# A scatter of mirrored rows that starts at partition 1 and moves 112 rows in place of 113

## The chip, the cores and the metric

The kernel runs on one core of a Trainium2 chip. The metric is the device time of one execution in microseconds. Before the change the median of three runs is 688.1 us (683.28 to 690.54).

## The reference

Eight batches, 12 heads, 448 rows, head width 64, model width 768, hidden width 3072. What is computed, cut to its core:

```python
scores = scale * np.matmul(q, k.transpose(0, 1, 3, 2))
attn = np.maximum(scores, 0.0) ** 2 / S
x = (attn @ v)                      # then heads side by side: (8, 448, 768)
X = np.fft.fft(np.fft.fft(x, axis=1), axis=2)
u = x + np.real(X)
un = (u - mean(u)) / np.sqrt(var(u) + 1e-06)
out = u + np.maximum(un @ w_ch1, 0.0) @ w_ch2
```

Inputs and output are float32; the kernel's matmuls take bfloat16.

## The kernel before

Work goes through eight batches b = 0 to 7. For each batch TensorE (PE) makes scores (`psS`, L734), ScalarE and VectorE turn them into squares (`sq`), PE multiplies by the values (L716), the result is copied to `xT`, folded, and sent through the Fourier matrices (L1210, L1024). Meanwhile PE works on the feed-forward part of earlier rows: first layer at L1445 (`hT <- unT, w`), second layer at L1496 and L1576, whose partial sums VectorE adds into the output tile `o` (L1431). The order of all instructions on each engine is fixed while the program is built, by a planner (`Streams.run`) that knows due times and costs; on the chip each engine then works through its list in that order, so an instruction that waits holds up everything behind it on its engine.

The Fourier result of a real signal is symmetric: rows s and 448 - s come from the same products. So `mix_rows` makes two tiles of rows at a time: `us[0]` holds rows s, `us[1]` holds their mirror images 448 - s. For batches 2 to 7 (`b >= PAR`) it goes over the even rows first (ch = 0, partition p is row 2p, 113 of them with rows 0 and 224) and then over the odd rows (ch = 1, 112 of them). The top half of a batch goes to `utop` (float32, for the output sum) and `ntop` (bfloat16, normalised, for the first layer); the mirrored half goes to `ubot` and `nbot`, in DRAM. Those tiles have 384 rows, of which 224 are used.

The mirrored rows come in reverse order, so they are written by a scatter: an indirect DMA issued by GpSimd (POOL) at L1120 in `store_rows`, whose destination row for each partition stands in a small index tile, `back2[ch]` (`backe` in the profile). The top rows go out by a plain DMA from SP at L1117. Partition 0 of the even mirrored tile is row 448, which is the mirror of row 0 and is not part of the output: its index is 224, an unused row.

From batch 1 on, the mirrored tile `u` has one buffer for both ch (`side` gives 1), and so do the `un` tiles. So the first instruction that writes the next `u` (POOL, L1057, then L1059) waits until the scatter out of that buffer has landed, and the next `un` (L1082 on POOL or L1085 on ACT) waits for the `nbot` scatter. Behind POOL's L1057 and L1059 stand the row statistics on VectorE (L1066), and behind those in VectorE's list the additions and copies that free PE's accumulators.

Before a batch's rows go to the first layer, SP reads them back transposed (`unT <- ntop`, `unT <- nbot`, L1158); SP's one list also holds the transposes of q and k (L481), of `xT` (L650), the loads `o <- utop`, `o <- ubot` (L1363) and the stores of the output (L1367).

Of the kernel before, what the change touches and what calls it, by code (L numbers as in the profile page):

```python
# [136 lines left out]
def need(eng, dur, deps=(), bufs=(), ok=None):  # L137
    return eng, dur, list(deps), list(bufs), ok
# [26 lines left out]
def kernel(  # L165
# [9 lines left out]
    nc = tc.nc  # L175
# [3 lines left out]
    R = S // 4  # L179
    HS = S // 2  # L180
# [12 lines left out]
    PAR, EV = 2, 113  # L193
# [39 lines left out]
    back2 = [const.tile([128, 1], mybir.dt.int32, name=f"backe{i}") for i in range(2)]  # L233
# [31 lines left out]
    def mirrors():  # L265
        order[0] = work.tile([128, 128], BF16, name="order", tag="qkr0", bufs=1)
        nc.gpsimd.memset(rev, 0.0)
        nc.gpsimd.affine_select(out=rev, in_=rev, compare_op=ALU.not_equal, fill=1.0,
                                base=-127, pattern=[[1, 128]], channel_multiplier=1)
        nc.gpsimd.iota(back[0], pattern=[[0, 1]], base=HS, channel_multiplier=-1)  # L270

        v = const.tile([128, 2], FP32, name="backv")
        nc.gpsimd.iota(v[:, 0:1], pattern=[[0, 1]], base=HS - 128, channel_multiplier=-1,
                       allow_small_or_imprecise_dtypes=True)
        nc.gpsimd.tensor_scalar(v[:, 1:2], v[:, 0:1], 0.0, float(UB), op0=ALU.is_lt, op1=ALU.mult)
        nc.gpsimd.tensor_tensor(v[:, 0:1], v[:, 0:1], v[:, 1:2], op=ALU.add)
        nc.gpsimd.tensor_copy(back[1], v[:, 0:1])
        for i in range(2):
            nc.gpsimd.iota(back2[i], pattern=[[0, 1]], base=HS - i, channel_multiplier=-2)
        nc.gpsimd.memset(order[0], 0.0)  # L280
        for i in range(2):
            n = EH - i
            nc.gpsimd.affine_select(out=order[0][:, i * EH:i * EH + n], in_=order[0][:, i * EH:i * EH + n],
                                    compare_op=ALU.not_equal, fill=1.0, base=-i, pattern=[[-2, n]],
                                    channel_multiplier=1)
        nc.gpsimd.tensor_scalar(order[0][:, EH - 1:EH], order[0][:, EH - 1:EH], 0.5, None, op0=ALU.mult)
# [75 lines left out]
    def load_group(i, which=(0, 1, 2)):  # L362
# [3 lines left out]
        for x, (nm, src) in enumerate((("q", q), ("k", k), ("v", v))):  # L366
            if x not in which:
                continue
            if b == 0 and x < 2:
                e = yield need("POOL", 0.85)  # L370
                t = first_qk[x][:R, g]
            else:
                e = yield need("POOL", 0.85, bufs=[BQ[x] if x == 2 else BQ[x][home(i)]])
                t = work.tile([R, HG, 4 * Dh], BF16, name=f"{nm}n",
                              tag="vn" if x == 2 else f"{nm}n{home(i)}", bufs=3 if x == 2 else 1)
            nc.gpsimd.dma_start(out=t, in_=src[b, hs].rearrange("h (p j) d -> p h (j d)", j=4))  # L376
            loads[i][x] = t.rearrange("p h (j d) -> p j h d", j=4)

            ready[i][x].t = sch.dma(e, GRP, 360e3, "sw") + (1.5 if g else 0.0, 3.0, 14.0, 7.0)[min(b, 3)]
            if i == 0 and x == 1:  # L380
                yield need("POOL", 0.7)
                make_identity(nc, ident)
            if i == 0 and x == 2:
                e = yield need("POOL", 1.1)
                dft_indices()
                indices_ready.t = e + LATENCY["POOL"]
            if i == 2 and x == 2:
                yield need("POOL", 0.75)
                pads()
            if i == NG + 1 and x == 1:  # L390
                yield need("POOL", 3.6)
                mirrors()
# [716 lines left out]
    def store_rows(b, ch, top, bot, us, nbytes, t, cells):  # L1109

        get = lambda u: u() if callable(u) else u
        s0, s1 = SC[ch]
        n = s1 - s0 if b < PAR else EV - ch
        w = min(128, HS - s0) if b < PAR else R
        if top is not None:
            e = yield need("SP", 0.1, [t[0]])
            nc.sync.dma_start(out=top[s0:s0 + w, :] if b < PAR else top[ch::2, :], in_=get(us[0])[:w])  # L1117
            cells[2 * ch].t = sch.dma(e, w * D * nbytes)
        e = yield need("POOL", 1.1, [t[1]])
        nc.gpsimd.indirect_dma_start(  # L1120
            out=bot, out_offset=bass.IndirectOffsetOnAxis(ap=(back if b < PAR else back2)[ch][:n], axis=0),
            in_=get(us[1])[:n], in_offset=None)
        cells[2 * ch + 1].t = sch.dma(e, w * D * nbytes) + 1.0

    def u_store(b, ch, us, ut, freed):
        yield from store_rows(b, ch, utop[b], ubot[b], us, 4, ut, u_stored[b])
        yield need("SP", 0.0, freed)
        for i in range(2):
            t = max(u_stored[b][2 * ch + i].t, freed[i].t)
            BU[i][side(b, ch)].free.append(t)  # L1130
            if b == ONE - 1 and ch == 0:
                u_left[i].t = t

    def n_store(b, ch, t):
        yield from store_rows(b, ch, ntop[b], nbot[b], [lambda i=i: uns[b][2 * ch + i] for i in range(2)], 2,
                              t, n_stored[b])
        if b > 0:
            BUN[0].free.append(n_stored[b][2 * ch + 1].t)
# [571 lines left out]
```

## Time and profile before

| | |
|---|---|
| median of three runs | 688.1 us (683.28 to 690.54) |
| the profiled execution | 686.53 us |
| its span, first to last instruction | 684.6 us |
| PE busy | 594.1 us |
| VectorE busy | 408.0 us |
| ScalarE busy | 331.2 us |
| GpSimd busy | 153.4 us |
| mean granted clock of TensorE | 0.945 |

Shares and chains below are of the profiled execution. Busy time of an engine counts instructions that run, not those that wait.

### The profile page before, as it was taken

Reading aid. Unit: us, or ns where it says so; the run is one execution under the profiler, and the core shown is the slowest. Engines: PE = TensorE matmul, PEld = TensorE weight load, DVE = VectorE, ACT = ScalarE, POOL = GpSimd, SP = SyncE. Lnnn points to the kernel's source line nnn. Section 1 sums busy time; section 2 is a strip of 40 time slices with the busy share of each in tenths; the row PEclk is TensorE's granted clock in tenths of the full one; section 3 lists DMA queues with packets and bytes.
Section 4 is the critical chain, followed back from the end, with each engine's and each line's share of the span. In section 5 each row is a group of like instructions: output and inputs, shape, how many; then the busy total and the mean of one; then the engine's idle time right before and its main releaser. Section 6 shows DMA issues by size and latency. Waiting matters only on the chain.

```text
span 684.6 us, 11457 instructions
## 1 busy us (share of the span) xinstructions
PE 594.1 (87%) x4476; PEld 371.7 (54%) x4476; DVE 408.0 (60%) x929; ACT 331.2 (48%) x503; POOL 153.4 (22%) x190
## 2 busy tenths in 40 slices
PE   8999999999748999479988699599689936999997
PEld 6575565444414455137645467258347724777684
DVE  6977779776547477366857576578546713232313
ACT  5858736765123577255575538366434302122130
POOL 8360314111232112331414133203300221000000
PEclk9999999999969899799998999899989977999999
DMA  9999997877359869999799959994783322312021
GB/s 134 210 217 224 223 141 180 116 120 110 99 72 134 153 133 63 73 158 189 117 76 128 223 110 88 144 200 94 37 148 86 90 75 57 111 35 81 24 70 47
DMA packets 141941, 81.96 MB, mean 120 GB/s; under 512 B 86054, under 2 KB 137158, under 8 KB 141888
## 3 DMA queue, kind: packets, MB, share of 16 engines
q1 hardware_dynamic: 93120, 47.50, 41.4%
q0 software_dynamic: 48768, 33.74, 34.0%
q8 instruction: 35, 0.57, 0.3%
q14 instruction: 18, 0.15, 0.1%
HBM read 62.91 MB, written 26.27 MB: 130 GB/s over the span
## 4 chain that ended last, share of the span: by engine, by line
PE 42%; DMA 28%; issue 16%; DVE 4%; POOL 4%; ACT 4%; SPq 2%; POOLq 0%; DVEq 0%; ACTq 0%
PE psF L1445 20%; DMA ubot<-u,backe 16%; PE psF L1576 10%; DMA nbot<-un,backe 7%; PE psF L1470 3%; PE psS L734 3%; PE psF L716 3%; ACT sq L759 2%; DMA qkT<-qkr 2%; DMA unT<-ntop 1%; DMA ntop<-un 1%; DMA o<-ubot 1%; POOL u L1057 1%; POOL u L1059 1%; DVE sq L774 1%
## 5 line engine op out<-in xcount | busy, mean ns | idle before, releaser
L1445 PE MATMUL psF<-unT,w 128*128 128x256 bf16 (+2 forms) x1728 | 238.9, 298 | 36.9 <-ACT hT L1419 17.1
L1445 PEld LDWEIGHTS <-w 128*128 128x128 bf16 x1728 | 169.7, 100 | 103.7 <-issue 37.3
L759 ACT ACTIVATE sq<-psS 112x896 bf16<-112x896 f32 x192 | 164.2, 917 | 57.1 <-PE psS L734 56.8
L1419 ACT ACTIVATE hT<-psF 128x512 bf16<-128x512 f32 (+3 forms) x166 | 86.0, 530 | 134.2 <-PE psF L1445 133.6
L1576 PEld LDWEIGHTS <-hT 128*128 128x128 bf16 x792 | 78.3, 100 | 77.3 <-issue 31.5
L774 DVE TENSOR_TENSOR sq<-sq 112x896 bf16<-112x896 bf16 x162 | 98.6, 623 | 20.7 <-ACT sq L759 19.6
L1576 PE MATMUL psF<-w,hT 128*128 128x384 bf16 x462 | 83.7, 333 | 3.5 <-DVE hT L1417 3.5
L1431 DVE TENSOR_TENSOR o<-psF,o 128x384 f32<-128x384 f32 x92 | 50.7, 551 | 48.5 <-PE psF L1576 42.1
L1066 DVE BATCH_NORM_STATS2 stats<-u 112x6 f32<-112x384 f32 (+2 forms) x56 | 29.1, 546 | 62.1 <-POOL u L1057 52.0
L734 PE MATMUL psS<-qkT 64*128 64x448 bf16 (+1 forms) x384 | 54.2, 373 | 5.6 <-DMA qkT<-qkr 3.6
L716 PE MATMUL psF<-sq,vn 112*64 112x448 bf16 x312 | 38.7, 372 | 14.2 <-DVE o L1431 14.2
L1576 PE MATMUL psF<-wsum,hT 128*128 128x384 bf16 x198 | 38.5, 347 | 14.5 <-DVE o L1431 14.5
L1057 POOL TENSOR_TENSOR u<-tp,xn 112x385 f32<-112x385 f32 (+2 forms) x14 | 12.8, 912 | 170.1 <-DVE tp L1039 86.8
L716 PEld LDWEIGHTS <-vn 112*64 112x64 bf16 x384 | 18.4, 112 | 42.0 <-issue 34.4
L1069 ACT ACTIVATE std<-mv,eps_t 112x1 f32<-112x1 f32 (+2 forms) x28 | 8.2, 295 | 67.7 <-DVE mv L1067 56.1
L553 DVE TENSOR_SCALAR xT<-psF 128x224 bf16<-128x224 f32 x56 | 19.2, 384 | 33.1 <-PE psF L716 33.0
L734 PEld LDWEIGHTS <-qkT 64*128 64x128 bf16 (+1 forms) x384 | 16.1, 103 | 35.0 <-issue 24.1
L376 POOL DMA_DIRECT2D qn<-in_q_dram x21 | 15.3, 731 | 85.0 <-DVE qkr L469 67.8
L1085 ACT ACTIVATE un<-u,nmr,rstd 113x768 bf16<-113x768 f32 (+2 forms) x20 | 20.1, 1022 | 23.2 <-DMA nbot<-un,backe 12.7
L376 POOL DMA_DIRECT2D vn<-in_v_dram x24 | 17.2, 718 | 58.3 <-PE psS L734 40.4
L1417 DVE TENSOR_SCALAR hT<-psF 128x512 bf16<-128x512 f32 (+3 forms) x38 | 20.4, 549 | 16.2 <-PE psF L1445 15.6
L771 ACT ACTIVATE sq<-sq 112x896 bf16<-112x896 bf16 x30 | 28.5, 954 | 0.5
(166 smaller groups left out, 658.8 us busy)
## 6 DMA issues: line engine op xcount, KB each, us to landing
out_dram<-o SPq DMA_DIRECT2D x56, 192.0 KB, 2.3
vn<-in_v_dram POOLq DMA_DIRECT2D x24, 224.0 KB, 8.0
qn<-in_q_dram POOLq DMA_DIRECT2D x21, 224.0 KB, 5.1
kn<-in_k_dram POOLq DMA_DIRECT2D x21, 224.0 KB, 7.4
w<-in_moe_w_ch_dram POOLq DMA_DIRECT2D x12, 384.0 KB, 13.9
w<-in_moe_w_ch_dram POOLq DMA_DIRECT2D x4, 1152.0 KB, 22.9
utop<-u SPq DMA_DIRECT2D x12, 336.0 KB, 5.8
o<-utop SPq DMA_DIRECT2D x16, 192.0 KB, 6.3
```

The costliest lines, as they stand in the source:

```text
L376: nc.gpsimd.dma_start(out=t, in_=src[b, hs].rearrange("h (p j) d -> p h (j d)", j=4))
L716: nc.tensor.matmul(av[h * Dh:(h + 1) * Dh, 0:S], lhsT=vn[:, c, h0 + h, :], rhs=sq[:, h, :], start=(c == 0), stop=(c == 3))
L734: nc.tensor.matmul(sc[:wide, h, 0:S].rearrange("k (c q) -> k c q", c=4), lhsT=flat[ps, k0:k0 + wide], rhs=qT[ps, m % 2], start=True, stop= ...
L759: nc.scalar.activation(r, sc[:R, :, 0:S], AF.Relu)
L771: nc.scalar.activation(r, r, AF.Square)
L774: nc.vector.tensor_tensor(r, r, r, op=ALU.mult)
L1066: nc.vector.bn_stats(stats[:n, hf, :], u[:n, hf * (D // 2):(hf + 1) * (D // 2)])
L1419: nc.scalar.activation(hs, ps, AF.Relu)
L1431: nc.vector.tensor_tensor(o, pc[:, 0:DH], o, op=ALU.add)
L1445: nc.tensor.matmul(ph[:, i * N:(i + 1) * N], lhsT=w1_sb[m][hf][:, (jj + i) * 128:(jj + i + 1) * 128], rhs=unT[:, m, 0:N], start=(m == 0), ...
L1470: nc.tensor.matmul(pc[:, 0:DH], lhsT=block(j, c), rhs=w2(j, hf), start=(j == 0), stop=(j == JC - 1))
L1576: nc.tensor.matmul(pc[:, 0:DH], lhsT=lhs[i], rhs=rhs[i], start=(start and i == 0), stop=(i == KP - 1), skip_group_check=True)
```

## The change

The even mirrored scatter leaves out partition 0, whose destination is the unused row. It reads partitions 1 to 112 of the tile, and since the index tile is read from its partition 0 on, its values are shifted by one row: 222 - 2p in place of 224 - 2p. For the odd rows the new expression gives the values that it gave before (223 - 2p), from partition 0, 112 rows. Both `ubot` and `nbot` go through this code, so in batches 2 to 7 it changes 12 scatters of 24. The rows of data that are used are the same, and so is the order of instructions on every engine.

```diff
         for i in range(2):
-            nc.gpsimd.iota(back2[i], pattern=[[0, 1]], base=HS - i, channel_multiplier=-2)
+            nc.gpsimd.iota(back2[i], pattern=[[0, 1]], base=HS - 2 + i, channel_multiplier=-2)
...
-        n = s1 - s0 if b < PAR else EV - ch
+        n, r0 = (s1 - s0, 0) if b < PAR else (R, 1 - ch)
...
             out=bot, out_offset=bass.IndirectOffsetOnAxis(ap=(back if b < PAR else back2)[ch][:n], axis=0),
-            in_=get(us[1])[:n], in_offset=None)
+            in_=get(us[1])[r0:r0 + n], in_offset=None)
```

Here `R` is 112, `HS` is 224, `EV` is 113 and `PAR` is 2.

## Rows read from the trace of the kernel before

**Rows 1.** The page, busy time, share of the span, instructions of each engine.

```profile
PE 594.1 (87%) x4476; PEld 371.7 (54%) x4476; DVE 408.0 (60%) x929; ACT 331.2 (48%) x503; POOL 153.4 (22%) x190
```

**Rows 2.** Chain that ended last, by line, shares of the span.

```profile
by line: PE psF L1445 20.2%; issue 16.0%; DMA ubot<-u,backe 15.5%; PE psF L1576 9.6%; DMA nbot<-un,backe 6.7%; PE psF L1470 2.7%; PE psS L734 2.7%; PE psF L716 2.7%; ACT sq L759 2.0%; DMA qkT<-qkr 1.7%; DMA unT<-ntop 1.4%; DMA ntop<-un 1.3%
```

**Rows 3.** Waits of POOL, then of VectorE: us in total, times, longest.

```profile
POOL u L1057 <- DMA ubot<-u,backe: 83.2, 6, 19.6
POOL un L1082 <- DMA nbot<-un,backe: 34.5, 4, 10.6
...
DVE stats L1066 <- POOL u L1057: 52.0, 6, 14.7
```

**Rows 4.** PE in order of time: start, us, instructions, [idle before <- releaser].

```profile
198.25 1.70 PE L716 MATMUL psF<-sq,vn 112*64 112x448 bf16 x8 [14.24 <-DVE o L1431]
...
223.92 2.08 PE L1445 MATMUL psF<-unT,w 128*128 128x384 bf16 x6 [3.78 <-DMA unT<-nbot]
...
286.11 4.00 PE L1576 MATMUL psF<-wsum,hT 128*128 128x384 bf16 x12 [10.06 <-DVE o L1431]
...
308.82 5.46 PE L1445 MATMUL psF<-unT,w 128*128 128x256 bf16 x36 [5.17 <-DMA unT<-ntop]
...
362.54 4.59 PE L1445 MATMUL psF<-unT,w 128*128 128x256 bf16 x24 [6.56 <-DVE xT L553]
...
431.03 2.99 PE L1576 MATMUL psF<-w,hT 128*128 128x384 bf16 x9 [3.50 <-DVE hT L1417]
...
445.14 3.59 PE L1576 MATMUL psF<-wsum,hT 128*128 128x384 bf16 x12 [4.41 <-DVE o L1431]
...
496.42 0.96 PE L716 MATMUL psS<-sq,vn 112*64 112x448 bf16 x4 [5.28 <-DVE sq L774]
505.50 2.08 PE L1445 MATMUL psF<-unT,w 128*128 128x256 bf16 x12 [2.67 <-DVE o L1431]
...
566.09 5.19 PE L1445 MATMUL psF<-unT,w 128*128 128x256 bf16 x24 [12.92 <-ACT hT L1419]
575.24 4.06 PE L1445 MATMUL psF<-unT,w 128*128 128x256 bf16 x24 [3.95 <-ACT hT L1419]
```

**Rows 5.** POOL in order of time around the first even scatter of batch 2.

```profile
173.58 2.43 POOL L1120 DMA_INDIRECT ubot<-u,backe  x1 [0.32 <-POOL u L1059]
195.24 0.90 POOL L1057 TENSOR_TENSOR u<-tp,xn 112x385 f32<-112x385 f32 x1 [19.23 <-DMA ubot<-u,backe]
...
199.83 1.04 POOL L1120 DMA_INDIRECT ubot<-u,backe  x1 [0.30 <-issue]
```

**Rows 6.** DMA issues (us to landing), 113 rows, issued near 173.6, 336.7, 489.9, 418.2.

```profile
ubot<-u,backe POOLq DMA_INDIRECT x1, 21.5
...
ubot<-u,backe POOLq DMA_INDIRECT x1, 22.5
...
nbot<-un,backe POOLq DMA_INDIRECT x1, 11.7
...
nbot<-un,backe POOLq DMA_INDIRECT x1, 21.6
```

**Rows 7.** The same, 112 rows, near 575.0, 375.6, 493.5; last batch 1's two.

```profile
nbot<-un,backe POOLq DMA_INDIRECT x1, 2.8
...
nbot<-un,backe POOLq DMA_INDIRECT x1, 6.7
...
ubot<-u,backe POOLq DMA_INDIRECT x1, 10.0
...
ubot<-u,back POOLq DMA_INDIRECT x2, 5.4
```

**Rows 8.** Busy by stretch: us, five engines, PEclk, DMA share of 16, GB/s.

```profile
190.00:195.00 5.00, 0.00 (x0) 0.00 (x0) 0.00 (x0) 0.00 (x0) 0.00 (x0) 0.50 0.06 26
```

**Rows 9.** The same, PE alone: first of ten stretches after idle, and sum.

```profile
198.25:202.40 4.15, 4.15 (x19) 0.50 0.49 122
...
505.50:509.63 4.13, 4.13 (x23) 0.59 0.59 179
...
sum 39.82, PE 39.81; mean PE 3.98
```

**Rows 10.** DMA issues from 255 to 285 us: transposes by SP in batch 3.

```profile
qkT<-qkr SPq DMA_TRANSPOSE x2, 14.5
```

## The prediction

> **What bounds the kernel now.** I read the busy table first: PE works for 594.1 us of a span of 684.6 us [rows 1], so some 90 us are PE waiting, and those are what an edit outside PE can win. The chain of waits then names a DMA where one would expect PE: the two scatters `ubot` and `nbot` of batches 2 to 7 hold 15.5% and 6.7% of the span [rows 2], together some 152 us. A share of the chain is not yet a saving, since PE works beside most of it. So I followed the wait down the engines. POOL waits 83.2 us in six pieces for `ubot`, always to overwrite the one `u` buffer, and 34.5 us for `nbot` to overwrite `un`; VectorE, whose next item is the statistics of that `u`, stands for 52.0 us in six pieces behind POOL [rows 3]. PE stops when VectorE no longer frees its accumulators: in the list of PE's idle gaps I count ten from 170 us on that hang on this [rows 4], among them 14.24, 10.06 and 12.92 us.
>
> Next, why a scatter takes so long. The even ones have 113 rows and land 20 to 22 us after issue (float32), or 11.7 us and once 21.6 us (bfloat16, half the bytes) [rows 6]. The odd ones, one row fewer and otherwise alike, land in 2.8 to 6.7 us (bfloat16), and in 10.0 us (float32) where they were issued 3.6 us behind an even `nbot` and land with it [rows 7]. A stretch where nothing else ran shows what the difference is: between 190 and 195 us all five engines are idle, the scatter is alone, and the DMA engines are busy for 0.06 of their sixteenfold time, moving 26 GB/s [rows 8]. 0.06 is one engine of sixteen. **113 rows go through one DMA engine**, 112 rows do not.
>
> **The rule beside it.** The Trainium skill, "DMA: Bandwidth & Descriptors", section on why a DMA increments its semaphore by 16 and not by 1, says that a transfer uses the largest number of engines up to 16 that divides the size of its slowest dimension. 113 is prime, so this gives one; 112 gives 16; the trace agrees for 113 with its 0.06. The same section names an exception on trn2, by which some copies issued from GpSimd spread over all engines with the count rounded up; by that 113 rows would already be spread and the sum below would be zero. The 0.06 of [rows 8] speaks against it here.
>
> **The change, part by part.**
>
> *The index tile.* One iota is replaced by another of the same shape: nothing. It is built in the first microseconds and the order of every engine is unchanged.
>
> *Issue.* An even scatter holds POOL for 2.43 us, an odd one for 1.04 us [rows 5]. Twelve even ones at odd price: 12 x 1.4 = 17 us of POOL. POOL is busy for 153 us in all [rows 1], and its time counts only through the waits below, so I add nothing for it.
>
> *Landing of the even `ubot`.* No scatter starting at partition 1 is in the trace, so this is bounded. Below: 2.8 us, an odd `nbot` of half the bytes. Above: 10.0 us, the odd `ubot` that lands together with a slow one. The nearest rows are the two of batch 1, float32 rows of the same width, 5.4 us [rows 7]. I take 7 us, since batches 2 to 7 have more transfers beside them. Should the start at partition 1 keep the scatter on one engine, it stays at 21.5; that is a rival.
>
> *What it frees.* About 14 us earlier landing, six times, is 84 us, more than the 52.0 us of VectorE's wait. Its longest piece, 14.7 us [rows 3], stands behind the scatter that took 21.5 us: it is gone at a landing under 21.5 - 14.7 = 6.8 us, so at 7 us 0.2 us remain, at 10 us 3.2 us. The other five share 37.3 us, 7.5 us each, and are gone at either.
>
> *Even `nbot`.* By the same rows, from 11.7 or more to about 4 us. It sits before the odd `un`, hence before the odd `nbot` and the transposed read of the rows.
>
> *PE's gaps.* Six follow the `ubot` scatter directly: 14.24, 10.06, 6.56, 3.50, 5.28 and 12.92 us = 52.6 us. Four follow from the later `un` and its transposes: 3.78 (`unT <- nbot`), 5.17 (`unT <- ntop`), 2.67 and 3.95 us = 15.6 us [rows 4]. Together **68.1 us**. I leave in place the 4.41 us gap at 445 us and smaller ones: there the last wait is a q/k transpose.
>
> *The clock.* After each of these gaps PE restarts at a granted clock of 0.50, the lower of its two levels (1.2 GHz in place of 2.4): ten stretches, 39.8 us of work, nine at about 0.50 and one at 0.59 [rows 9]. At full clock the same work takes half of it, less 0.4 us for the one: **19.5 us**.
>
> *Given back.* What is late next is SP's list. In batch 3 the q/k transposes already take 14.5 us to land [rows 10], and the two gaps on `unT` (3.78 + 5.17 us) end on transposes. I let half of these two stay, 4.5 us, with 2 us of slow clock behind them, and 1.5 us for the residue of `ubot`: **8 us**.
>
> Sum, from the profiled execution's own 686.5 us (span 684.6): 686.5 - 68.1 - 19.5 + 8 = **607 us**. That execution is 1.6 us under the median of 688.1, which is inside the spread of the three runs. With no gap given back it would be 599; if the small gaps went too, some 590. I take 607, with 592 to 622 as this case's own range.
>
> **The rivals.**
>
> 1. *Only the direct waits go.* The scatter spreads, but SP's queue is what comes next: the four following gaps stay, and each batch gains a new wait of 2 us on a transpose. For it: rows 10, and that the scatter now uses all the engines that the transposes use. Against: other stretches with the same list of work show PE nearly without gaps, and the planner's order assumed quick scatters. Time: 686.5 - 52.6 - 15 (their part of the clock, 52.6/68.1 of 19.5) + 12 = 631 us. Chance 0.17.
>
> 2. *It doesn't spread.* The start at partition 1, or the shifted pairing of index and row, leaves the scatter on one engine, or the count wasn't the reason. Then nothing but one row in 113 is saved: 0.2 us of each landing, 686 us. Against it stands that the odd scatters differ in nothing else but the count. Chance 0.05. The Trainium skill's exception, above, would give the same time.
>
> 3. *Slower.* Spread over all sixteen engines, an even scatter gets ahead of q/k and `xT` transposes on every engine instead of one, and the score matmuls (L734), which wait for them, stop PE. To lose, each of the twelve changed scatters must cost PE more than 87.6 / 12 = 7.3 us; at 8 us each it would be 686.5 - 87.6 + 96 = 695 us. Against: 20 us on one engine is 1.3 us on sixteen. The gaps of that kind now are few, the 4.41 us one among them [rows 4]. Chance 0.03.
>
> The forecast has 0.72; the 0.03 left are for times under 592, where the small gaps go too.
>
> **Range and chances.** 590 to 636 us: from the forecast's lower end with the small gaps, to rival 1 with a landing of 10 us (3 to 5 us more). Runs spread by about half a per cent each way, so 1%, some 7 us, is what tells a change from none. Faster by over 1%: the forecast, rival 1 and the low tail, 0.92. Within 1%: rival 2, 0.05. Slower: 0.03.
>
> **What would show it.** Right: even scatters issue in about 1.0 us and land in under 8 us (float32) and 5 us (bfloat16); the row of POOL waiting for `ubot` falls from 83.2 to under 25 us, VectorE's 52.0 to a few; the gaps of 14.24, 10.06 and 12.92 us are absent; PE busy falls to some 575 us since its work keeps the upper clock; the scatters leave the head of the chain and PE's lines lead it. Rival 1 would show gaps that end on `unT`, `qkT` or `xn`. Wrong altogether: a stretch with 0.06 of the DMA engines during an even scatter, or an issue that still takes 2.4 us. The weakest step is the size of what is given back, since each engine's fixed order can turn one late transfer into a new stop.

## The result and the profile after

The changed kernel takes 588.38 us (median of six runs, 585.95 to 590.88) against 688.81 us (six runs, 683.28 to 692.54): a ratio of 0.8546, 95% interval 0.8503 to 0.8588. The forecast was 607 us with a range of 590 to 636: the direction came out, and so did the mechanism by which the scatters were slow; the time lies 1.6 us under the range, and the gain is 100 us where 80 were forecast.

The page after, busy time of each engine in a span of 586.3 us; it answers to [rows 1]:

```profile
PE 571.7 (98%) x4476; PEld 364.4 (62%) x4476; DVE 412.8 (70%) x929; ACT 330.2 (56%) x503; POOL 137.6 (23%) x190
```

PE's busy time falls by 22.4 us with the same 4476 matmuls, and the time in which it does nothing falls from 684.6 - 594.1 = 90.5 us to 14.6 us. The two make up the whole difference of the spans, 98.3 us. The chain of waits, which had the two scatters at 15.5% and 6.7% [rows 2], now reads:

```profile
by line: PE psF L1445 33.9%; PE psF L1576 23.5%; PE psS L734 5.5%; PE psF L716 4.5%; PE psF L1496 4.0%; PE psF L1470 3.2%; PE psS L1210 2.5%; DVE sq L774 2.3%; ACT sq L759 2.0%; DMA xn<-xT 1.9%; PE psS L716 1.2%; DMA qkT<-qkr 1.1%; issue 1.
```

No scatter is left in it; PE's lines lead. The same place that [rows 5] showed, POOL around the first even scatter of batch 2 (start, us, instruction, idle before and what ended it):

```profile
174.13 1.01 POOL L1120 DMA_INDIRECT ubot<-u,backe  x1 [0.28 <-POOL u L1059]
180.84 0.91 POOL L1057 TENSOR_TENSOR u<-tp,xn 112x385 f32<-112x385 f32 x1 [5.71 <-ACT un L1085]
```

The even scatter issues in 1.01 us (2.43 before) and POOL writes the next `u` at 180.84 us, 6.7 us after the issue, where it had waited until 195.24. What it waits for last is now ACT's `un`, not the DMA; the waits of POOL for `ubot` and `nbot` in [rows 3] are gone from its list. The scatters' landing (median us; even and odd ones together, 16.7 and 9.2 before):

```profile
ubot<-u,backe POOLq DMA_INDIRECT x12, 5.0
nbot<-un,backe POOLq DMA_INDIRECT x12, 5.0
```

Of the even `ubot` scatters three have a landing in the trace: 4.7, 5.7 and 6.0 us.

And PE in the stretch of the 14.24 us gap of [rows 4], in order of time:

```profile
175.66 8.94 PE L1496 MATMUL psF<-w,hT 128*128 128x384 bf16 x54
184.53 0.95 PE L716 MATMUL psF<-sq,vn 112*64 112x448 bf16 x8
```

The eight value matmuls follow at once, and take 0.95 us where they took 1.70 at the lower clock. From 54 us on, PE's largest gap in the whole execution is 1.26 us. PE's waits by cause, the two longest:

```profile
PE psS L1654 <- DVE warm L258: 1.3, 1, 1.3
PE psF L1445 <- DVE hT L1417: 1.3, 1, 1.3
```

No line of this view names a DMA any more. The mean granted clock is 0.999 (0.945 before).

### The profile page after: what moved, and what is told of

It is laid out like the page before. It is cut to its first block, busy times and chain, and to the rows that moved or that the text cites. A ratio compares the mean times of both kernels' runs of the same rounds, so it can differ in the third digit from the quotient of the medians.

```text
span 586.3 us, 11457 instructions
## 1 busy us (share of the span) xinstructions
PE 571.7 (98%) x4476; PEld 364.4 (62%) x4476; DVE 412.8 (70%) x929; ACT 330.2 (56%) x503; POOL 137.6 (23%) x190
## 4 chain that ended last, share of the span: by engine, by line
PE 82%; DVE 8%; ACT 4%; DMA 3%; SPq 1%; issue 1%; POOL 0%; DVEq 0%; POOLq 0%
PE psF L1445 34%; PE psF L1576 24%; PE psS L734 6%; PE psF L716 4%; PE psF L1496 4%; PE psF L1470 3%; PE psS L1210 2%; DVE sq L774 2%; ACT sq L759 2%; DMA xn<-xT 2%; PE psS L716 1%; DMA qkT<-qkr 1%; PE psS L821 1%; PE psS L1024 1%; SPq L1158 1%
## 5 line engine op out<-in xcount | busy, mean ns | idle before, releaser
L1445 PE MATMUL psF<-unT,w 128*128 128x256 bf16 (+2 forms) x1728 | 229.3, 291 | 4.8 <-DVE hT L1417 1.3
L1445 PEld LDWEIGHTS <-w 128*128 128x128 bf16 x1728 | 165.6, 98 | 65.8 <-issue 13.5
L774 DVE TENSOR_TENSOR sq<-sq 112x896 bf16<-112x896 bf16 x162 | 102.4, 646 | 16.3 <-ACT sq L759 15.2
L1576 PEld LDWEIGHTS <-hT 128*128 128x128 bf16 x792 | 76.1, 98 | 54.2 <-issue 5.8
L1576 PE MATMUL psF<-w,hT 128*128 128x384 bf16 x462 | 81.5, 326 | 0.3 <-DVE hT L1417 0.2
L734 PE MATMUL psS<-qkT 64*128 64x448 bf16 (+1 forms) x384 | 51.4, 358 | 1.6 <-ACT sq L759 0.6
L716 PE MATMUL psF<-sq,vn 112*64 112x448 bf16 x312 | 37.0, 358 | 0.0
L1576 PE MATMUL psF<-wsum,hT 128*128 128x384 bf16 x198 | 35.0, 326 | 0.0
L716 PEld LDWEIGHTS <-vn 112*64 112x64 bf16 x384 | 17.7, 109 | 21.2 <-issue 13.5
L1470 PE MATMUL psF<-w,hT 128*128 128x384 bf16 x144 | 25.1, 326 | 0.0
```

The costliest lines, as they stand in the source:

```text
L716: nc.tensor.matmul(av[h * Dh:(h + 1) * Dh, 0:S], lhsT=vn[:, c, h0 + h, :], rhs=sq[:, h, :], start=(c == 0), stop=(c == 3))
L734: nc.tensor.matmul(sc[:wide, h, 0:S].rearrange("k (c q) -> k c q", c=4), lhsT=flat[ps, k0:k0 + wide], rhs=qT[ps, m % 2], start=True, stop= ...
L774: nc.vector.tensor_tensor(r, r, r, op=ALU.mult)
L1445: nc.tensor.matmul(ph[:, i * N:(i + 1) * N], lhsT=w1_sb[m][hf][:, (jj + i) * 128:(jj + i + 1) * 128], rhs=unT[:, m, 0:N], start=(m == 0), ...
L1470: nc.tensor.matmul(pc[:, 0:DH], lhsT=block(j, c), rhs=w2(j, hf), start=(j == 0), stop=(j == JC - 1))
L1576: nc.tensor.matmul(pc[:, 0:DH], lhsT=lhs[i], rhs=rhs[i], start=(start and i == 0), stop=(i == KP - 1), skip_group_check=True)
```

## The experiments

Two theories of where the gain comes from. **A**: the scatters were waited for, by the next `u` and `un` in the same buffers. **B**: a scatter on one DMA engine holds that engine for some 20 us, and every transfer that is spread over all engines, transposes above all, finishes only when that one does. The reason ahead of both, that the row count sets the number of engines, is tested by a series of counts.

### One scatter at a time

The edit keeps 113 rows for one of the two (here `nbot`; the other kernel has `== 4`), with an index tile `full` that holds the old values:

```diff
+        whole_rows = b >= PAR and ch == 0 and nbytes == 2
+        if whole_rows:
+            n, r0 = EV, 0
...
```

> Even float32 scatter (ubot) 112 rows from partition 1, even bfloat16 scatter (nbot) left at 113 rows. Theory A (the waits to overwrite u and un): the six direct gaps go (52.6 us) with their part of the slow clock (15 us), the four gaps behind un stay: 618 to 625 us. Theory B (a scatter that holds one DMA engine of sixteen slows every other transfer, and that is what mattered): nbot holds the engine a third of the time that both did, so a third of the 100 us comes back: about 621 us, with q/k transposes that still land in over 8 us. Both: the ubot scatter lands in 5 to 8 us, POOL's wait on nbot grows above 34 us.

> Even bfloat16 scatter (nbot) 112 rows, even float32 scatter (ubot) left at 113 rows. Theory A: POOL still waits some 80 us for ubot, the six direct gaps stay, the four behind un go (15.6 us and 4 us of clock): 660 to 670 us. Theory B: ubot holds the engine two thirds of the time, so about 655 us.

With 112 rows for `ubot` alone: 623.89 us, ratio 0.9062 (0.9019 to 0.9104). For `nbot` alone: 653.31 us, ratio 0.9475 (0.9441 to 0.9509). The first fits both theories, but what was expected of it beside the time came only in part: POOL's wait for `nbot` fell to 13.9 us in place of growing above 34, and the q/k transposes land in 5.5 us in the median, where theory B wanted over 8. The second lies outside A's 660 to 670 and near B's 655. In its profile POOL still waits as long as before for `ubot`:

```profile
POOL u L1059 <- DMA ubot<-u,backf: 86.5, 6, 19.8
```

and PE's 14.24 us gap of batch 2 is there in full (14.37 us), yet 36 us are won. A's price of 15.6 + 4 us for the `nbot` part was half of it. In the profile of the other kernel, with `ubot` spread, two of PE's four longest waits by cause are these:

```profile
PE psF L1450 <- DMA unT<-ntop: 5.8, 1, 5.8
...
PE psF L1450 <- DMA unT<-nbot: 4.2, 1, 4.2
```

They end on transposed reads. They are there while `nbot` has 113 rows, and gone when it has 112. The two gains add up, 65 + 36 = 101 us against 100 together.

### A scatter that nobody waits for

The changed kernel, with a spare scatter out of a weight tile that is only read into a scratch tensor, so nothing waits for its buffer:

```diff
+        if b >= PAR and ch == 0 and nbytes == 4:
+            nc.gpsimd.indirect_dma_start(
+                out=spare, out_offset=bass.IndirectOffsetOnAxis(ap=full[:113], axis=0),
+                in_=w1_sb[0][0][:113], in_offset=None)
...
```

The control has 112 in both places; the late version has the condition `ch == 1 and nbytes == 2`.

> The changed kernel, and after each even ubot scatter one more scatter of 113 rows of 3 KB, out of a weight tile into a scratch tensor that nobody reads; nothing waits for it. Theory A: POOL pays 2.4 us six times and nothing else, 588 to 594 us. Theory B: one DMA engine is held for about 20 us six times, the nbot scatters, transposes and loads behind it land 10 us later or more and PE's gaps return: 605 us or more.

> The same with a spare scatter of 112 rows: the control for issue time and bytes. Both theories: 588 to 593 us, the spare scatter issues in 1.0 us and lands in 5 to 8 us.

> The changed kernel with the same spare scatter of 113 rows, now issued after each batch's last scatter (odd nbot), so that no scatter of that batch stands behind it on the one DMA engine; loads of q, k, v and SP's transposes still share that engine. Theory B1 (what costs is the queue of scatters behind a scatter on one engine): 588 to 598 us. Theory B2 (what costs is that transposes and loads, which use all sixteen engines, finish with the slowest): about as the early spare scatter, 615 us or more, with VectorE waiting some 20 us for q/k transposes.

With 113 spare rows: 634.74 us, ratio to the kernel before 0.9195 (0.9156 to 0.9234). With 112: 587.6 us, 0.8531 (0.8492 to 0.8569), the same as without. One row more in a transfer that nobody reads costs 47 us; the longer issue on POOL, 1.4 us six times, can be 8 of them at most. Late, with no scatter of the batch behind it: 648.8 us, 0.9474 (0.9398 to 0.9551), 61 us more than the control (they ran at different times; by the ratios it is 65) and worse than early, with VectorE waiting for q/k transposes for 42.3 us in place of the expected 20. So A falls as the only cause, and so does B1: in the early version the spread `nbot` scatter behind the spare one did land in 13.8 us or more in each batch, but taking it out of that place makes nothing better.

What it is shows in the late version's chain of waits, first from 185 to 220 us (start, us, what); the spare scatter is issued at 192.44 us and lands 19.7 us later, at 212.1:

```profile
195.61 18.95 DMA unT<-nbot
...
214.70 2.08 PE psF L1452 x6
```

The transposed read of the rows, issued 3 us after the spare scatter, lands 2.4 us after it; PE waits 10.3 us for it. PE's waits by cause in the same kernel:

```profile
PE psS L737 <- DMA qkT<-qkr: 23.2, 2, 12.6
PE psF L1452 <- DVE xT L556: 14.1, 2, 13.5
PE psF L1452 <- DMA unT<-nbot: 10.3, 1, 10.3
```

Three causes, two of them transposes by name, make 47.6 us of idle PE, where the kernel without the spare scatter has no wait on a DMA. Behind the third, a wait of 13.5 us that ends at 445.7 us, the chain from 425 to 447 us finds SP (SPq is its queue) and a q/k transpose; a spare scatter was in flight from 418.7 to 438.8 us:

```profile
428.60 7.57 SPq L1165
...
436.22 7.52 DMA qkT<-qkr
```

Here the held engine works in a second way: L1165 is SP issuing a transposed read, and the issue itself takes 7.57 us, so the q/k transpose behind it in SP's list starts late. The longest such issue is 12.33 us in the late version, 7.20 in the kernel before, 3.16 with 112 spare rows and 3.46 in the changed kernel; the 76 transposes from 165 us on take SP 167.4, 136.7, 108.5 and 105.8 us.

The kernel before has the same, without any spare scatter. From 165 us on, the 24 transposes that SP issued while an even scatter was in flight landed in 10.7 us in the median (5.3 to 18.7), the other 52 in 4.2 us (2.3 to 9.6). Of the 24, 23 landed after the scatter did, by 0.4 to 7.5 us; one landed 7.6 us ahead of it, so a transpose is not held in every case.

### How many rows

Even scatters of other counts, from partition 0 with the old index values; small stores at the start put zeros where rows are left out, the same in all six kernels:

```diff
...
-        n = s1 - s0 if b < PAR else EV - ch
+        n = s1 - s0 if b < PAR else (106, R)[ch]
```

> Even scatters move partitions 0 to 111 (112 rows from partition 0, with the unused row, without the last used one, which is filled with zeros at the start by small stores; the same stores are in all kernels of this series). If the row count decides: as the changed kernel, 586 to 594 us, ubot lands in 4 to 8 us. If the start at partition 1 or leaving out the unused row decides: 680 us or more.

> 111 rows from partition 0 (3 x 37; two used rows are left out). If the largest divisor up to 16 sets the number of DMA engines: 3 engines, 37 rows each, ubot lands in 7 to 10 us, time 590 to 610 us. If every count that is no multiple of 16 goes through one engine: 680 us or more. If the rows are spread with the count rounded up: as 112 rows.

> 106 rows from partition 0 (2 x 53). By divisors: 2 engines, 53 rows each, ubot lands in 10 to 13 us, time 600 to 630 us, between the two kernels. One engine for all that is no multiple of 16: 680 us or more. Rounded up: as 112 rows.

> 109 rows from partition 0 (a prime). By divisors: one engine as with 113, ubot lands in 19 to 22 us, time 675 to 690 us, though it moves fewer rows than the changed kernel. If it was the row beyond 112: as 112 rows, under 595 us.

> Even scatters move 104 rows from partition 0 (8 x 13; the used rows beyond are left out, zeros in their place). Largest divisor up to 16: 13 engines of 8 rows, ubot lands in 4 to 7 us and the time is that of 112 rows, 588 to 594 us. If only powers of two counted: 8 engines of 13 rows, 5 to 8 us, hardly slower. If only multiples of 16: 680 us.

> 108 rows (12 x 9). Largest divisor: 12 engines of 9 rows, ubot lands in 4 to 7 us, 588 to 594 us. If only powers of two counted: 4 engines of 27 rows, ubot lands in 7 to 9 us and POOL waits for it some 10 to 25 us, 592 to 600 us.

| rows | largest divisor up to 16 | issue of the first, us | `ubot`, us to landing (even ones read) | time, us | ratio to before |
|---|---|---|---|---|---|
| 109 | 1 | 2.38 | 18.8 to 21.4 | 684.31 | 0.9935 (0.9895 to 0.9975) |
| 106 | 2 | 1.63 | 10.4 and 12.6 | 603.89 | 0.878 (0.8715 to 0.8846) |
| 111 | 3 | 1.43 | 10.4 to 11.7 | 600.18 | 0.8726 (0.8656 to 0.8796) |
| 108 | 12 | 1.06 | 4.4 to 6.2 | 592.3 | 0.8637 (0.8549 to 0.8725) |
| 104 | 13 | 1.07 | 4.6 to 6.1 | 589.05 | 0.8589 (0.85 to 0.8679) |
| 112 | 16 | 1.01 | 3.5 to 5.8 | 589.74 | 0.8575 (0.851 to 0.8639) |

109 rows, fewer than the changed kernel moves, are as slow as 113; 112 from partition 0, with the unused row in, are as fast as the change. So neither the start at partition 1 nor the unused row matters, and the count alone does. One expectation was missed: 111 rows should have landed in 7 to 10 us and took 10.4 to 11.7, no less than 106 rows on two engines; why isn't shown. The engines can be counted where a scatter is nearly alone. Stretches of one us with 109, 106 and 111 rows in flight (us, PE busy, PEclk, DMA share, GB/s):

```profile
193.00:194.00 1.00, 0.00 (x0) 0.50 0.07 29
```

```profile
183.00:184.00 1.00, 1.00 (x9) 1.00 0.12 49
```

```profile
182.00:183.00 1.00, 1.00 (x9) 1.00 0.16 66
```

One sixteenth is 0.06, two are 0.12, three 0.19: one engine at 29 GB/s, two at 49, and for 111 rows more than two and not quite three. The Trainium skill's rule in "DMA: Bandwidth & Descriptors", section on why a DMA increments its semaphore by 16 and not by 1, the largest divisor up to 16, agrees with all six counts. The exception that the Trainium skill names in the same section is for some direct copies; these scatters are indirect, and none of them shows it. Two engines already give back 85 of the 100 us. What the times of 104 and 108 rows tell is less sharp: 592.3 us for 108 fits 12 engines and 4, the landing speaks for 12 (4.4 to 6.2 us where 7 to 9 were expected for 4), and 104 rows with 13 or 8 engines would look alike. The packets, in the last section, tell these apart.

## Why the prediction was wrong in size

**What bounds the kernel: right, but not the whole.** PE's idle time was the thing to win, and the wait went down from the scatter over POOL and VectorE to PE, as the 14.37 us gap shows that stays with `ubot` at 113 rows. What the prediction has nowhere is the second path, from the held engine over the transposes to PE; the spare scatters, which nobody waits for, cost 47 to 61 us by it.

**113 rows on one engine, 112 on sixteen: right**, shown by the counts above. Rival 2 is out.

**Issue: right** (2.43 to 1.01 us).

**Landing: taken too long.** The even `ubot` scatters take 4.7 to 6.0 us where it can be read, not 7, near the 5.4 of [rows 7]; I had moved away from the nearest row for transfers alongside, without a row for it. One of "the other five" waits of VectorE was 12.1 us and not 7.5; at this landing it is gone all the same.

**PE's gaps: right for the ten, wrong for the rest.** I priced 68.1 us and put the 4.41 us gap at 445 us and smaller ones at nothing, "there the last wait is a q/k transpose". Idle PE fell by 75.9 us: the ten are gone and so are those of 4.41, 3.61 and 1.57 us, and 3.2 us in smaller gaps are what remains from 170 us on. The transpose behind the 4.41 us gap was itself a slow one. SP issued it at 423.44 us, while the even `nbot` scatter of 418.21 us ([rows 6], 21.6 us) was in flight; the issue took 7.20 us, the landing 18.7, and VectorE waited for it ahead of the work that PE needed (SP's issue, its landing, VectorE):

```profile
423.44 7.20 SPq L481 DMA_TRANSPOSE qkT<-qkr  x1
...
qkT<-qkr SPq DMA_TRANSPOSE x1, 18.7
...
442.27 0.43 DVE L469 COPY qkr<-kn 112x1024 bf16<-112x1024 bf16 x1 [5.24 <-DMA qkT<-qkr]
```

**Given back, 8 us: this step failed.** It said that SP's list is late next and let half of the two gaps on `unT` stay, with slow clock behind them. Nothing was given back. I took the transposes' long landing, 14.5 us in batch 3 [rows 10], for a limit of their own that a spread scatter would press on. Those two landed in 11.1 and 17.8 us and were issued 1.6 and 2.9 us after an even `ubot` scatter; with no scatter beside them the transposes of the same trace take 4.2 us in the median. The spare scatters show that this is cause and not chance: one held engine takes a transposed read to 18.95 us, and the same bytes on sixteen engines cost nothing (587.6 us). So the row that I used against the change was a symptom of what the change removes. Rival 1, which kept the following gaps, was priced on the same mistake; the trace of before had the numbers against it.

**The clock: right in kind, low by 3 us.** 19.5 us were forecast, less 2 us in the deduction; PE's busy time fell by 22.4 us. The gaps that I left in place had slow stretches behind them as well: the twelve matmuls at 445.14 us took 3.59 us [rows 4], and twelve of that kind take 2.11 us after the change.

In numbers, the 18.7 us between the sum of 606.9 and the profiled execution's 588.24 us are three terms: the 8 us given back that were not, 7.8 us of idle PE that I had put at nothing (75.9 - 68.1), and 2.9 us of slow clock behind it (22.4 - 19.5). The lower end of the range, 590, was 599 with some 9 us for the small gaps and nothing for the slow clock behind them; those 2.9 us are more than the 1.6 us by which the time lies under it. The case that happened, the small gaps gone too, stands in the prediction as the low tail, with a chance of 0.03.

**Rival 3** is out by the 112-row spare scatter: six more scatters on sixteen engines leave the time where it was.

Open is how the 100 us divide between the wait for the buffers and the held engine: in the kernel before both came from the same transfers. The held engine alone is enough for 47 to 61 us, by the spare scatters. For the wait alone no run gives a figure; that it counts shows in the 14.24 us gap of batch 2, where for 5 us nothing but the scatter was at work [rows 8]. A kernel with 113 rows and a second `u` buffer, which would take away the first alone, wasn't tried.

## What to carry to other kernels

Look at the row count of every indirect DMA: its largest divisor up to 16 is the number of DMA engines that it got in all counts tried here, and a prime like 113 or 109 got one. One row fewer, to a multiple of 16, was worth 100 of 689 us here with the order of instructions unchanged, and two engines already won 85 of them. A slow transfer also has to be looked for behind the waits of others: while one engine is held, transposes look slow by themselves, in landing and in issue, and a forecast that takes their time as given counts the gain too low.

## What was not expected of the hardware

The issue of a scatter on GpSimd gets longer with fewer engines, not with more rows: 2.38 us for 109 rows on one engine, 1.63 for 106 on two, 1.43 for 111 on three, 1.01 for 112. And the count of packets on the software queue goes with it; the kernel before and after:

```profile
q0 software_dynamic: 48768, 33.74, 34.0%
...
q0 software_dynamic: 40320, 33.63, 37.4%
```

The bytes are the same to about 0.1 MB, so on average 704 more packets go with each of the twelve scatters on one engine. The size that the trace holds for each packet tells what kind they are: before, each even `ubot` scatter has 840 packets of 8 bytes and each even `nbot` scatter 555 of 12 and 15 of 8 bytes; after, the queue has none of either size.

Their number goes with the engines that get no rows. With 113 rows one engine of sixteen works, fifteen are left, and the 840 are 15 x 56. With 109 rows the count in an even `ubot` scatter is 810 = 15 x 54, with 106 rows 378 = 14 x 27, with 111 rows 234 = 13 x 18, with 108 rows 16 = 4 x 4, with 104 rows 15 = 3 x 5 (12 = 3 x 4 in one batch of six), and with 112 rows none. This settles what the landing left open: 15 and 12 are no multiples of the 8 engines that would be left if 104 rows used eight, and 16 is none of the 12 that would be left if 108 rows used four. What these packets are for the runs don't show.
